# A linear attention followed by a rational feed-forward layer: groups of four d_ff slices by 512 tokens, and the q stage issued beside the MoE stage

## Chip, cores, metric

One core of a Trainium2 chip. The metric is the device time of one execution in microseconds (us), the median of several runs; the profile is of one such run. Engines: PE (TensorE matmul), PEld (its weight loads), DVE (VectorE), ACT (ScalarE), POOL (GpSimd), SP (issues DMAs). "Clock" is the TensorE clock that was granted, as a share of full speed. A "table load" brings a set of function tables to ACT before an Ln or an Exp.

## The reference

```python
# q, k, v: (4 batches, 4 heads, 1088, 32); S1, S2: (8, 32)
phi(x)  = outer(S1 x, S2 x), flattened to 64 features
kv, z   = sum over s of phi(k) v^T, and of phi(k)
x       = (phi(q) kv) / (phi(q) z + 1e-6)          # heads side by side: (4352, 128)
h       = x @ w_in                                  # (4352, 2048)
P       = a0 + a1 h + a2 h^2 + a3 h^3
Q       = 1 + |b0||h| + |b1| h^2
out     = (P / (Q + 1e-6)) @ w_out                  # (4352, 128)
```

## The kernel before

Three stages: k (builds kv for every batch), q (builds x transposed, xT, in SBUF), then MoE (the feed-forward part) over token tiles of 1024. The q stage holds six PSUM banks, which go back before the MoE stage takes eight. The division by Q is Ln and then Exp of the negative, both on ACT. A framework orders each engine's instructions and places their waits; the order on an engine is fixed in the program but is not the order of the source.

```python
    for b in range(B):                                  # the q stage
        for si in range(n_stiles):                      # 9 tiles of 128 tokens
            # load q, transpose (PE), copy (ACT), project (PE), copy (ACT), outer product (DVE)
            for hp in range(H // 2):
                # transpose q_p (PE), copy (ACT), multiply by kv into nd_ps (PE)
                for j in range(2):
                    nc.scalar.copy(out=xT[...], in_=nd_ps[off:off + D, :sl])
                    nc.vector.tensor_copy(out=denb[...], in_=nd_ps[off + D:off + D + 1, :sl])
        for c0 in range(bt0, bt0 + S, CW):              # normalise, 512 tokens at a time
            # reciprocal of denb (DVE), spread over heads (PE, rden_ps), xT *= rden_ps (DVE)
    attn_stack.close()                                  # PSUM of the q stage is given back
    # ... moe_ps 1 x [128,1024] f32, moe_ps_h 2 x [128,1024] f32, moe_ps_t 2 banks
    TT = 1024
    while t0 < n_tok:
        for fi in range(nf):                            # 16 slices of d_ff
            h_ps = moe_ps_h.tile([128, TT], FP, name="h_ps")
            for c0 in range(0, tl, 512):
                nc.tensor.matmul(h_ps[:, c0:c0 + cl], lhsT=w_in_sb[:, fi * 128:(fi + 1) * 128],
                                 rhs=xT_t[:, c0:c0 + cl], start=True, stop=True)
            nc.scalar.copy(out=hh[:, :tl], in_=h_ps[:, :tl])
            # DVE: h2, t1, P3, P (two steps), Qp (two steps)
            nc.scalar.activation(out=habs[:, :tl], in_=hh[:, :tl], func=ACT.Abs, scale=ab0)
            nc.scalar.activation(out=Qln[:, :tl], in_=Qp[:, :tl], func=ACT.Ln, bias=one_ap)
            nc.scalar.activation(out=Qr[:, :tl], in_=Qln[:, :tl], func=ACT.Exp, scale=-1.0)
            nc.vector.tensor_mul(out=g[:, :tl], in0=P[:, :tl], in1=Qr[:, :tl])
            # PE: out_ps += w_out slice @ g; at the end of the tile copy, transpose, copy, store
```

## Time and profile before

| | before |
|---|---|
| time, median | 824.9 us (824.6 to 825.9, 13 runs) |
| k stage, q stage, MoE stage | to 92, 92 to 305, 305 to 823 us |
| ACT busy | 594.5 of 822.9 us |
| table loads on ACT | 159 of 1.283 us |

Two lines of the page of the kernel before: busy us of each engine with its share of the span, and the chain of work that ended last, by engine. They are averages over three stages with different limits; the prediction below takes the stages apart.

```profile
PE 471.7 (57%) x1204; PEld 230.8 (28%) x1212; DVE 422.3 (51%) x892; ACT 594.5 (72%) x905; POOL 9.9 (1%) x55
...
ACT 57%; PE 21%; issue 11%; DVE 8%; DMA 2%; SPq 0%; ACTq 0%
```

ACT leads both, but 72% would suggest much more slack than the MoE stage has.

### The profile page before, as it was taken

Reading aid. Unit: us, or ns where it says so; the run is one execution under the profiler, and the core shown is the slowest. Engines: PE = TensorE matmul, PEld = TensorE weight load, DVE = VectorE, ACT = ScalarE, POOL = GpSimd, SP = SyncE. Lnnn points to the kernel's source line nnn. Section 1 sums busy time; section 2 is a strip of 40 time slices with the busy share of each in tenths; the row PEclk is TensorE's granted clock in tenths of the full one; section 3 lists DMA queues with packets and bytes.
Section 4 is the critical chain, followed back from the end, with each engine's and each line's share of the span. In section 5 each row is a group of like instructions: output and inputs, shape, how many; then the busy total and the mean of one; then the engine's idle time right before and its main releaser. Section 6 shows DMA issues by size and latency. Waiting matters only on the chain.

```text
span 822.9 us, 5049 instructions
## 1 busy us (share of the span) xinstructions
PE 471.7 (57%) x1204; PEld 230.8 (28%) x1212; DVE 422.3 (51%) x892; ACT 594.5 (72%) x905; POOL 9.9 (1%) x55
## 2 busy tenths in 40 slices
PE   3888965665565546555545556554666546533431
PEld 2767733333333222111112111111222212111210
DVE  0111344345434446666566665665656666566333
ACT  2222433332332219999999999999999999999997
POOL 3000000000000000000000000000000000000000
PEclk9999999999999997757676877777555577765555
DMA  6333210000000000000000000000000000000000
GB/s 147 59 59 58 34 28 13 8 11 13 5 0 1 0 0 0 1 0 0 0 6 20 0 1 0 0 20 6 0 0 2 13 13 0 0 0 1 19 7 6
DMA packets 59869, 11.34 MB, mean 14 GB/s; under 512 B 54848, under 2 KB 59200, under 8 KB 59712
## 3 DMA queue, kind: packets, MB, share of 16 engines
q1 hardware_dynamic: 59840, 11.02, 7.1%
q8 instruction: 10, 0.16, 0.1%
q14 instruction: 19, 0.16, 0.1%
HBM read 8.79 MB, written 2.23 MB: 13 GB/s over the span
## 4 chain that ended last, share of the span: by engine, by line
ACT 57%; PE 21%; issue 11%; DVE 8%; DMA 2%; SPq 0%; ACTq 0%
ACT L245 12%; ACT L247 11%; ACT Qln L245 10%; ACT Qr L247 8%; ACT hh L229 7%; PE nd_ps L183 5%; PE kv L134 4%; DVE denb L197 3%; PE ab_ps L126 3%; ACT xT L188 3%; DVE denb L190 3%; ACT habs L237 2%; PE rden_ps L199 2%; PE q_pT L175 2%; PE ab_ps L165 2%
## 5 line engine op out<-in xcount | busy, mean ns | idle before, releaser
L226 PE MATMUL h_ps<-xT,w_in_sb 128*128 128x512 f32 (+1 forms) x288 | 221.7, 892 | 140.2 <-ACT hh L229 139.1
L249 DVE TENSOR_TENSOR g<-P,Qr 128x1024 bf16<-128x1024 bf16 (+1 forms) x80 | 49.0, 612 | 194.8 <-ACT Qr L247 194.8
L226 PEld LDWEIGHTS h_ps<-xT,w_in_sb 128*128 128x128 f32 x288 | 74.5, 280 | 250.6 <-ACT hh L229 207.4
L188 ACT COPY xT<-nd_ps 32x128 f32<-32x128 f32 (+1 forms) x144 | 35.9, 249 | 105.0 <-PE nd_ps L183 77.9
L252 PE MATMUL out_ps<-g,w_out_sb 128*128 128x512 bf16 (+1 forms) x136 | 62.6, 542 | 83.4 <-DVE g L249 83.1
L245 ACT ACT_TABLE_LOAD x79 | 101.4, 1283 | 1.4
L247 ACT ACT_TABLE_LOAD x79 | 101.4, 1283 | 1.4
L190 DVE COPY denb<-nd_ps 1x128 f32<-1x128 f32 (+1 forms) x144 | 40.6, 282 | 84.5 <-ACT xT L188 83.0
L245 ACT ACTIVATE Qln<-Qp,one_ap 128x1024 bf16<-128x1024 bf16 (+1 forms) x80 | 81.5, 1020 | 2.3 <-DVE Qp L243 1.4
L237 ACT ACTIVATE habs<-hh,b_abs 128x1024 bf16<-128x1024 bf16 (+1 forms) x80 | 80.6, 1008 | 0.1
L247 ACT ACTIVATE Qr<-Qln 128x1024 bf16<-128x1024 bf16 (+1 forms) x80 | 74.2, 928 | 0.9
L229 ACT CAST hh<-h_ps 128x1024 bf16<-128x1024 f32 (+1 forms) x80 | 68.8, 868 | 5.6 <-PE h_ps L226 5.6
L183 PE MATMUL nd_ps<-q_pT_sb,kv_blk 128*128 128x128 f32 (+1 forms) x144 | 52.3, 467 | 21.3 <-DVE denb L190 21.3
L252 PEld LDWEIGHTS <-w_out_sb 128*128 128x128 bf16 x144 | 18.6, 131 | 133.5 <-issue 131.8
L130 DVE TENSOR_TENSOR k_p<-ab_sb 128x256 f32<-128x256 f32 (+1 forms) x36 | 15.3, 424 | 75.1 <-ACT ab_sb L128 75.1
L231 DVE TENSOR_TENSOR h<-hh 128x1024 bf16<-128x1024 bf16 (+1 forms) x80 | 48.4, 605 | 5.6 <-ACT hh L229 5.6
L183 PEld LDWEIGHTS nd_ps<-q_pT_sb,kv_blk 128*128 128x128 f32 x144 | 38.6, 321 | 39.1 <-PE q_pT L175 24.4
L175 PE MATMUL q_pT<-ident,q_p 128*128 128x128 f32 (+1 forms) x72 | 33.0, 458 | 28.7 <-ACT q_pT_sb L179 28.1
L243 DVE TENSOR_TENSOR Qp<-Qp,habs 128x1024 bf16<-128x1024 bf16 (+1 forms) x80 | 48.4, 605 | 0.7 <-ACT habs L237 0.6
L240 DVE TENSOR_TENSOR P<-P,t 128x1024 bf16<-128x1024 bf16 (+1 forms) x80 | 48.4, 605 | 0.0
L239 DVE TENSOR_TENSOR P<-P,h 128x1024 bf16<-128x1024 bf16 (+1 forms) x80 | 48.4, 604 | 0.0
L233 DVE TENSOR_SCALAR t<-hh,a_sb 128x1024 bf16<-128x1024 bf16 (+1 forms) x80 | 40.1, 501 | 0.0
(56 smaller groups left out, 468.1 us busy)
## 6 DMA issues: line engine op xcount, KB each, us to landing
out_dram<-outT_sb SPq DMA_DIRECT2D x34, 64.0 KB, 1.6
k_sb<-in_k_dram SPq DMA_DIRECT2D x32, 64.0 KB, 2.3
v_aug<-in_v_dram SPq DMA_DIRECT2D x32, 64.0 KB, 2.1
q_sb<-in_q_dram SPq DMA_DIRECT2D x32, 64.0 KB, 2.0
w_in_sb<-in_moe_w_in_dram SPq DMA_DIRECT2D x1, 1024.0 KB, 5.6
k_sb<-in_k_dram SPq DMA_DIRECT2D x4, 32.0 KB, 2.2
v_aug<-in_v_dram SPq DMA_DIRECT2D x4, 32.0 KB, 2.2
q_sb<-in_q_dram SPq DMA_DIRECT2D x4, 32.0 KB, 2.2
```

The lines of the kernel that those rows point to most:

```text
L175: nc.tensor.transpose(q_pT[:, :sl], in_=q_p[:sl, 2 * hp:2 * hp + 2, :, :].rearrange("s h i j -> s (h i j)"), identity=ident[:sl, :sl])
L183: nc.tensor.matmul(nd_ps[:, :sl], lhsT=kv_blk_sb[:, blk0:blk0 + wblk], rhs=q_pT_sb[:, :sl], start=True, stop=True)
L188: nc.scalar.copy(out=xT[h * D:(h + 1) * D, tok0:tok0 + sl], in_=nd_ps[off:off + D, :sl])
L190: nc.vector.tensor_copy(out=denb[h * D:h * D + 1, tok0:tok0 + sl], in_=nd_ps[off + D:off + D + 1, :sl])
L226: nc.tensor.matmul(h_ps[:, c0:c0 + cl], lhsT=w_in_sb[:, fi * 128:(fi + 1) * 128], rhs=xT_t[:, c0:c0 + cl], start=True, stop=True)
L229: nc.scalar.copy(out=hh[:, :tl], in_=h_ps[:, :tl])
L231: nc.vector.tensor_mul(out=h2[:, :tl], in0=hh[:, :tl], in1=hh[:, :tl])
L237: nc.scalar.activation(out=habs[:, :tl], in_=hh[:, :tl], func=ACT.Abs, scale=ab0)
L245: nc.scalar.activation(out=Qln[:, :tl], in_=Qp[:, :tl], func=ACT.Ln, bias=one_ap)
L247: nc.scalar.activation(out=Qr[:, :tl], in_=Qln[:, :tl], func=ACT.Exp, scale=-1.0)
L249: nc.vector.tensor_mul(out=g[:, :tl], in0=P[:, :tl], in1=Qr[:, :tl])
L252: nc.tensor.matmul(out_ps[:, c0:c0 + cl], lhsT=w_out_sb[:, fi, :], rhs=g[:, c0:c0 + cl], start=(fi == 0), stop=(fi == nf - 1))
```

## The change

Its intent: fewer, longer instructions on ACT and DVE (and fewer table loads) in the MoE stage, and MoE work of one batch beside the q work of the next. The PSUM is split anew so that both fit in eight banks: four for q, one shared by the normalisation and the output transposes, one out_ps, two h_ps of 512.

```diff
-    attn_stack = ExitStack()
-    attn_ps = attn_stack.enter_context(tc.tile_pool(name="attn_ps", bufs=1, ...PSUM))
+    attn_ps = ctx.enter_context(tc.tile_pool(name="attn_ps", bufs=1, ...PSUM))
...
-    attn_ps3 = attn_stack.enter_context(tc.tile_pool(name="attn_ps3", bufs=2, ...PSUM))
+    attn_ps3 = ctx.enter_context(tc.tile_pool(name="attn_ps3", bufs=1, ...PSUM))
...
+    TT = 512
+    def do_moe(t0, tl):
+        NJ = 4
+        for f0 in range(0, nf, NJ):
+            hh = moe_tmp.tile([128, NJ, TT], BF, name="hh")
+            for j in range(NJ):
+                h_ps = moe_ps_h.tile([128, TT], FP, name="h_ps")
+                nc.tensor.matmul(h_ps[:, :tl], lhsT=w_in_sb[:, (f0 + j) * 128:(f0 + j + 1) * 128], ...)
+                nc.scalar.copy(out=hh[:, j, :tl], in_=h_ps[:, :tl])
+            # the same DVE and ACT operations as before, each once over [128, NJ, tl]
...
+    def do_q(b):       # the body of the q loop, unchanged
...
-    attn_stack.close()
+    done = 0
+    do_q(0)
+    for b in range(B):
+        if b + 1 < B:
+            do_q(b + 1)
+        while done < n_tok and min(done + TT, n_tok) <= (b + 1) * S:
+            do_moe(done, min(TT, n_tok - done))
+            done += TT
```

## The prediction

> **What bounds the kernel now.** I read the table of engines by stretches first. It splits the 822.9 us into three stages. The columns are PE, PE weight load, VectorE (DVE), ScalarE (ACT) and GpSimd busy us with instruction counts, then the granted PE clock.
>
> ```profile
> 60.00:80.00 20.00, 17.59 (x105) 14.21 (x105) 3.82 (x9) 4.95 (x22) 1.04 (x10) 1.00 0.37 57
> ...
> 92.00:305.00 213.00, 127.15 (x352) 76.87 (x352) 95.15 (x215) 67.59 (x290) 0.00 (x0) 1.00 0.06 10
> ...
> 310.00:740.00 430.00, 243.86 (x392) 84.25 (x398) 275.81 (x501) 425.78 (x403) 0.00 (x0) 0.69 0.01 4
> ```
>
> The k stage (to 92 us) is PE's, 88% busy. In the q stage (92 to 305 us) nobody is full: PE 60%, DVE 45%, ACT 32%; it is a chain of small steps. In the MoE stage (305 to 823 us) ACT is busy 425.8 of 430 us, 99%. So there ACT's work is the time, and PE has room at a clock of 0.69.
>
> Next the time-ordered view of ACT in the MoE stage: one period, from one Exp to the next, takes 406.80 - 400.04 = 6.76 us.
>
> ```profile
> 400.04 1.06 ACT L247 ACTIVATE Qr<-Qln 128x1024 bf16<-128x1024 bf16 x1
> 401.00 0.99 ACT L229 CAST hh<-h_ps 128x1024 bf16<-128x1024 f32 x1
> 402.01 1.28 ACT L245 ACT_TABLE_LOAD   x1
> 403.30 1.15 ACT L245 ACTIVATE Qln<-Qp,one_ap 128x1024 bf16<-128x1024 bf16 x1
> 404.36 1.13 ACT L237 ACTIVATE habs<-hh,b_abs 128x1024 bf16<-128x1024 bf16 x1
> 405.51 1.28 ACT L247 ACT_TABLE_LOAD   x1
> ```
>
> Two table loads are 2.56 us of the 6.76, and they compute nothing. The order is not the source's: the cast of a later step stands between Exp and Ln, so the steps are already interleaved. Then the groups with shapes kept apart (busy us, mean ns), for two points on the length of each operation:
>
> ```profile
> L245 ACT ACT_TABLE_LOAD x79 | 101.4, 1283 | 1.4
> L247 ACT ACT_TABLE_LOAD x79 | 101.4, 1283 | 1.4
> L245 ACT ACTIVATE Qln<-Qp,one_ap 128x1024 bf16<-128x1024 bf16 x64 | 73.5, 1148 | 2.2 <-DVE Qp L243 1.4
> ...
> L237 ACT ACTIVATE habs<-hh,b_abs 128x1024 bf16<-128x1024 bf16 x64 | 72.7, 1135 | 0.1
> ...
> L229 ACT CAST hh<-h_ps 128x1024 bf16<-128x1024 f32 x64 | 63.3, 996 | 5.6 <-PE h_ps L226 5.6
> ...
> L245 ACT ACTIVATE Qln<-Qp,one_ap 128x256 bf16<-128x256 bf16 x16 | 8.0, 507 | 0.2
> ```
>
> **What the Trainium skill says.** (1) "ScalarE: Activation LUTs", What ACT_TABLE_LOAD costs: 1283 ns a load plus about 1380 ns of drain, 2.66 us a switch. The trace agrees on 1283 and not on the drain: the load at 402.01 starts 0.02 us after the cast before it ends, and Ln starts 0.01 us after the load. I count 1.28 us. (2) The same section gives an ACTIVATE a fixed part (186 ns, about 93 more for each pointer operand) plus 0.833 ns an element, and says that back-to-back ones overlap by about 93 ns. The trace: Ln rises (1148-507)/768 = 0.835 ns an element with 293 ns fixed, and Exp at 400.04 overlaps the cast by 0.10 us. (3) "VectorE: DVE Perf Modes", The TRN2 errata: a fixed cost an instruction, so fewer, longer ones pay it less often. The trace: a bf16 product takes 685 ns at 1024 and 286 at 256, so 153 fixed and 0.52 an element. (4) "TensorE: Matmul & The Clock Gate", The HAM clock gate: half rate after idle windows, full rate after sustained work. The trace shows clocks from 0.50 to 1.00; one 512-wide f32 step (two instructions) takes 1.06 us at full clock (20 instructions in 10.61 us at 305 us) and 2.08 us at the low one (at 402.05).
>
> **The change, part one: bigger groups in the MoE stage.** Before, a step is 1024 tokens by one of 16 slices of d_ff: 5 token tiles (the last of 256) make 80 steps. After, a group is 512 tokens by four slices: 9 token tiles (the last of 256) by 4 are 36 groups, 32 of 2048 elements and 4 of 1024. The casts from PSUM stay one for each 512-wide matmul, 128 + 16 of them. By line through two points:
>
> - Table loads: 158 become 72 (one Ln and one Exp a group), 72 x 1.283 = 92 us, from 203.
> - Ln: 1148 + 1024 x 0.835 = 2003 ns; 32 x 2.003 + 4 x 1.148 = 69 us, from 81.5.
> - Exp: 1911 ns by the same line from 1056 and 415; 65 us, from 74.
> - Abs: 1983 ns from 1135 and 499; 68 us, from 81.
> - Casts: (996-358)/768 = 0.831 an element gives 571 ns at 512; 128 x 0.571 + 16 x 0.358 = 79 us, from 69. This part costs 10 us.
> - Output copies: 14 us, from 13.
>
> Sum 387 us against 521: 134 us less of ACT, 110 of them table loads. A full group on ACT is 4 x 0.571 + 1.983 + 2.003 + 1.911 + 2.566 = 10.75 us for what took two steps or 13.5 us.
>
> On DVE the five products become 42 us each (1217 ns at 2048), the two scale-and-adds 28 each, the scaling 26: 290 us, from 358. A group is 8.4 us of DVE. On PE nothing shrinks: a group has four f32 steps and four bf16 ones (0.29 us at full clock, 0.53 low), 5.4 us at full clock and 10.4 us at half.
>
> **Part two: q work beside MoE work.** The q stage of batch b+1 is now issued ahead of the MoE tiles of batch b, and PSUM is shared out so that both fit. The first normalised chunk (the multiplication into xT) ends at 123 us in the trace before, so MoE work could start there instead of at 305. From 123 to 305 us ACT is busy only 53.5 of 182 us. So after 123 us ACT has 53.5 + 387 = 440 us to do. With no gap it would end at 563, and with the drain of the last group (Exp, product, matmul, copies, transfer: 822.9 - 817.8 = 5 us before) near 570 us.
>
> I don't believe in no gap. Between two batches there are 1088/512 = 2.1 tiles, 8.5 groups: ACT 8.5 x 10.75 + 17 (a batch's q copies, 67.6/4) = 108 us; DVE 8.5 x 8.4 + 24 = 95 us; PE 8.5 x 5.4 + 32 = 78 us at full clock, about 120 with the MoE part at half clock. Three engines are near full, in a fixed order on each. And q is a chain through all three: each half of a tile goes matmul, copy on ACT, copy on DVE, twice, about 2.9 us alone (53 us / 18). Beside 2 us operations on ACT I estimate one more us for each wait on ACT and 0.4 on DVE, so 5.7 us a half and 102 us a batch. That is just the 108 us in which ACT does the MoE work; a little slower, and ACT runs out of MoE work before the next batch is ready. I take ACT at 88% over the three overlapped batches, some 330 us of its work (375 us), and 95% over the last 110 (116 us): 123 + 375 + 116 = 614, less some 10 us for the 0.1 us overlaps of casts that now follow one another, plus 5 of drain. That makes **610 us**.
>
> **The rivals.** (A) **PE becomes the bound.** h_ps shrinks from two buffers of 1024 to two of 512, so PE can run only two matmuls ahead of four casts. At half clock the third and fourth cast each wait 2.08 - 0.57 = 1.5 us: 3 us a group, 36 x 3 = 108 us more, if the casts stand together. For it: the clock is 0.50 at times when PE is busy 6 to 8 of 10 us (580 to 640 us). Against: the order puts single casts between Ln and Exp, and denser work should lift the clock; at 1.00 in the q stage PE does as much. It would make 660 to 700 us. (B) **The overlap fails**: q and MoE merely alternate, because q's chain is stretched or waits for PSUM or for the order on PE. Then the k and q stages keep their 305 us and the MoE stage takes 387 less 10: 690 us. Against: the trace before already mixes the normalisation of one batch with the copies of the next on the same tensors, so the dependence is by slice and not by tensor. (C) **Everything fits** and ACT never waits: 570 us. (D) The loads don't fall, or the groups lose the interleaving, so Ln waits for a DVE chain of about 7 us in each group: 36 x 4 us or more. Two buffers of each tile speak against it, as before.
>
> **Range and chances.** Even where the overlap gives nothing, the loads alone take the time to about 690; only A and B together come near 825. I centre between C and B, nearer to C: 610 us, 570 to 665 for 8 in 10. Faster by over 2% is 0.97, within 2% 0.02, slower 0.01.
>
> **What would show it.** Right: 70 to 73 table loads in all; Ln, Exp and Abs near 2.00, 1.91 and 1.98 us; casts of 0.57 us; ACT busy near 460 us of the span, from 594.5; the first h_ps matmul at 115 to 135 us; PE and DVE busy beside ACT between 130 and 450 us. Wrong: ACT idle for h_ps by tens of us (A); the MoE work starting only after 250 us, or stretches near the ends of batches where ACT is a third busy (B); over 85% ACT in all stretches after 130 us, which would put the time below 590 (C); ACT idle for the Qp of DVE (D).

## The result, and the profile after

631.0 us (629.2 to 632.2, 8 runs) against 824.9. The ratio of the changed kernel to the one before is 0.765 (95% interval 0.764 to 0.7655). Ratios here are the mean time of one kernel's fast runs over that of the other's of the same rounds, so not quite the ratio of the medians quoted.

The same two lines of the page after:

```profile
PE 386.1 (62%) x1200; PEld 205.3 (33%) x1212; DVE 382.7 (61%) x540; ACT 463.7 (74%) x755; POOL 9.9 (2%) x55
...
ACT 52%; PE 36%; DVE 6%; issue 4%; DMA 1%; SPq 0%; ACTq 0%
```

ACT has lost 131 us of work and still leads, but PE's part of the chain has risen from 21% to 36%. The groups with shapes kept apart (busy us, mean ns, then the idle time just before) show where ACT's work went:

```profile
L172 ACT CAST hh<-h_ps 128x512 bf16<-128x512 f32 x128 | 72.6, 586 | 44.5 <-PE h_ps L170 43.9
L180 ACT ACTIVATE habs<-hh,b_abs 128x2048 bf16<-128x2048 bf16 x32 | 64.1, 2004 | 0.3
L188 ACT ACTIVATE Qln<-Qp,one_ap 128x2048 bf16<-128x2048 bf16 x32 | 64.1, 2002 | 2.4 <-DVE Qp L186 2.0
...
L190 ACT ACTIVATE Qr<-Qln 128x2048 bf16<-128x2048 bf16 x32 | 61.1, 1910 | 0.4
...
L188 ACT ACT_TABLE_LOAD x36 | 46.2, 1283 | 0.6
L190 ACT ACT_TABLE_LOAD x36 | 46.2, 1283 | 0.6
```

There are 72 loads in groups, 92.4 us, where there were 158 and 202.8. The last column of the first line is new: the casts wait 43.9 us for h_ps, where before it was 5.6 us in all. The table of stretches after 123 us (where MoE work can begin) shows the cost. Its columns are the length, PE, PEld, DVE, ACT and POOL busy us, the clock, the DMA share and GB/s.

```profile
123.00:500.00 377.00, 230.84 (x583) 106.19 (x592) 274.72 (x376) 318.95 (x477) 0.00 (x0) 0.75 0.03 6
500.00:627.00 127.00, 62.20 (x141) 27.76 (x144) 78.97 (x99) 106.62 (x120) 0.00 (x0) 0.72 0.03 10
```

ACT is busy 425.6 of 504 us, 84%, so 78 us of it idle. What it waited for, as the view of waits has it for 123 to 500 us (us in total, times, longest):

```profile
ACT hh L172 <- PE h_ps L170: 37.3, 37, 2.6
ACT xT L246 <- PE nd_ps L241: 7.3, 10, 3.8
ACT out_sb L198 <- PE out_ps L195: 3.5, 3, 1.2
```

For the rest of the span the wait for h_ps is 10.9 us more: 48 of the 78 us. Finally, the time-ordered view of ACT in the overlapped stage (start us, length, instruction):

```profile
309.48 2.00 ACT L188 ACTIVATE Qln<-Qp,one_ap 128x2048 bf16<-128x2048 bf16 x1
311.50 0.26 ACT L246 COPY xT<-nd_ps 32x128 f32<-32x128 f32 x1
311.78 1.28 ACT L190 ACT_TABLE_LOAD   x1
313.07 1.91 ACT L190 ACTIVATE Qr<-Qln 128x2048 bf16<-128x2048 bf16 x1
315.01 0.25 ACT L246 COPY xT<-nd_ps 32x128 f32<-32x128 f32 x1
...
315.32 1.05 ACT L172 CAST hh<-h_ps 128x512 bf16<-128x512 f32 x2
```

The small q copies sit between the long MoE operations: between these two, ACT spent 3.2 us on a load and an activation, and a q copy that came ready in that time had to wait. In the last line two casts follow each other, which will matter below.

### The profile page after: what moved, and what is told of

Same layout as the page of the kernel before. It is cut to its first block, busy times and chain, and to the rows that moved or that the text cites. A ratio compares the mean times of both kernels' runs of the same rounds, so it can differ in the third digit from the quotient of the medians.

```text
span 627.1 us, 4385 instructions
## 1 busy us (share of the span) xinstructions
PE 386.1 (62%) x1200; PEld 205.3 (33%) x1212; DVE 382.7 (61%) x540; ACT 463.7 (74%) x755; POOL 9.9 (2%) x55
## 4 chain that ended last, share of the span: by engine, by line
ACT 52%; PE 36%; DVE 6%; issue 4%; DMA 1%; SPq 0%; ACTq 0%
PE h_ps L170 14%; ACT Qln L188 11%; ACT Qr L190 10%; ACT L190 7%; ACT L188 6%; PE kv L133 6%; ACT hh L172 5%; ACT habs L180 5%; PE out_ps L195 4%; PE ab_ps L125 4%; ACT xT L246 3%; PE nd_ps L241 2%; ACT q_pT_sb L237 2%; PE kT_ps L116 1%; PE q_pT L233 1%
## 5 line engine op out<-in xcount | busy, mean ns | idle before, releaser
L170 PE MATMUL h_ps<-xT,w_in_sb 128*128 128x512 f32 (+1 forms) x288 | 184.2, 749 | 48.7 <-ACT hh L172 47.1
L172 ACT CAST hh<-h_ps 128x512 bf16<-128x512 f32 (+1 forms) x144 | 78.1, 562 | 48.9 <-PE h_ps L170 48.2
L188 ACT ACTIVATE Qln<-Qp,one_ap 128x2048 bf16<-128x2048 bf16 (+1 forms) x36 | 68.6, 1907 | 2.4 <-DVE Qp L186 2.0
L180 ACT ACTIVATE habs<-hh,b_abs 128x2048 bf16<-128x2048 bf16 (+1 forms) x36 | 68.7, 1908 | 0.4
L192 DVE TENSOR_TENSOR g<-P,Qr 128x2048 bf16<-128x2048 bf16 (+1 forms) x36 | 41.9, 1165 | 39.6 <-ACT Qr L190 39.1
L190 ACT ACTIVATE Qr<-Qln 128x2048 bf16<-128x2048 bf16 (+1 forms) x36 | 65.3, 1815 | 0.4
L174 DVE TENSOR_TENSOR h<-hh 128x2048 bf16<-128x2048 bf16 (+1 forms) x36 | 41.8, 1161 | 8.2 <-ACT hh L172 7.8
L186 DVE TENSOR_TENSOR Qp<-Qp,habs 128x2048 bf16<-128x2048 bf16 (+1 forms) x36 | 41.6, 1155 | 1.1 <-ACT habs L180 0.9
L183 DVE TENSOR_TENSOR P<-P,t 128x2048 bf16<-128x2048 bf16 (+1 forms) x36 | 41.8, 1161 | 0.4
L182 DVE TENSOR_TENSOR P<-P,h 128x2048 bf16<-128x2048 bf16 (+1 forms) x36 | 41.6, 1157 | 0.3
```

Source lines behind the costliest of these rows:

```text
L170: nc.tensor.matmul(h_ps[:, :tl], lhsT=w_in_sb[:, (f0 + j) * 128:(f0 + j + 1) * 128], rhs=xT_t[:, :tl], start=True, stop=True)
L172: nc.scalar.copy(out=hh[:, j, :tl], in_=h_ps[:, :tl])
L174: nc.vector.tensor_mul(out=h2[:, :, :tl], in0=hh[:, :, :tl], in1=hh[:, :, :tl])
L180: nc.scalar.activation(out=habs[:, :, :tl], in_=hh[:, :, :tl], func=ACT.Abs, scale=ab0)
L183: nc.vector.tensor_add(out=P[:, :, :tl], in0=P[:, :, :tl], in1=t1[:, :, :tl])
L188: nc.scalar.activation(out=Qln[:, :, :tl], in_=Qp[:, :, :tl], func=ACT.Ln, bias=one_ap)
```

## The experiments

Each kernel ran beside the kernel before on the same chip, in three rounds; all gave a correct result. Each edit is to the changed kernel unless said otherwise.

### The two parts alone

**groups_h2** and **groups_h6**: bigger groups, no overlap.

```diff
+    for b in range(B): do_q(b)
+    attn_stack.close()              # q's PSUM given back, as before the change
+    moe_ps_h: bufs=2 (groups_h2) or bufs=6 (groups_h6), each [128, 512]; moe_ps_t: bufs=1
+    for t0 in range(0, n_tok, TT): do_moe(t0, min(TT, n_tok - t0))
-    (the look-ahead loop)
```

> Part one alone: the bigger MoE groups, but all q work first and the MoE stage after it as in the kernel before, with h_ps still two buffers of 512. Theory (ACT sets the MoE time, and casts wait for h_ps because only two matmuls can run ahead): MoE work on ACT about 377 us at some 87% busy, so 433 us after 305, in all about 735 us, with 40 us or more of ACT waiting for h_ps. Rival 1 (those waits come only from q work on PE, so without it ACT is 98% busy): about 695 us. Rival 2 (the loads saved bring nothing alone): over 800 us.

> As groups_h2 with six h_ps buffers in place of two, which PSUM has room for when no q work runs. Theory (the depth of h_ps makes the casts wait): the waits for h_ps fall under 15 us and the time is about 695 us, some 40 less than groups_h2. Rival (PE's rate at its low clock, or the order, makes them wait): within 10 us of groups_h2.

Measured: 743.2 us (ratio 0.900) and 694.7 us (0.842). The stretches of the MoE stage and the wait for h_ps in it, first groups_h2, then groups_h6:

```profile
305.00:741.00 436.00, 243.81 (x468) 91.67 (x466) 272.79 (x289) 373.58 (x367) 0.00 (x0) 0.74 0.02 5
...
ACT hh L169 <- PE h_ps L167: 51.8, 40, 2.5
```

```profile
305.00:691.00 386.00, 233.19 (x467) 89.98 (x466) 269.98 (x289) 368.89 (x367) 0.00 (x0) 0.73 0.02 6
...
ACT hh L169 <- PE h_ps L167: 5.5, 4, 4.3
```

ACT's work is nearly the same, the PE clock too; four more buffers take 46 us of waits and 49 us of time away. So more buffers take the wait away at the same clock: with two, PE can't work ahead while ACT is in its long operations. Nor is it that a kinder order parted the casts: in groups_h6 four in a row, at 498.54 us, don't wait. (That the rate of PE plays no part does not follow; bf16_h below shows that it does.) The pair also shows that the h_ps wait needs no q work: it is there without any.

**overlap_nj2**: the overlap alone, with groups the size of the old steps.

```diff
-        NJ = 4
+        NJ = 2
```

> Part two alone: the overlap of q and MoE work as in the changed kernel, with groups of 1024 elements (two slices of d_ff by 512 tokens), the size of a step before, so 144 table loads. Theory: ACT has 185 us of loads and about 508 us of MoE work in all, and 54 of q work after 123 us, 562 us at some 90% busy: about 745 us. Rival (PE and the q chain set the pace of the overlapped stage, not ACT): the table loads cost less than their length there, and the time is under 700 us.

Measured: 732.1 us (0.887), a little under the 745 expected; ACT is busy 539.7 of the 607 us after 123, 89%. The rival (under 700) falls. With two casts a group, and the same two buffers and the same matmul, ACT's wait for h_ps is only 4.8 us. The overlap alone is worth 93 us, the groups alone with the same two buffers 82, and together they are worth 194, 19 more than the sum. "Alone" isn't quite clean: with 512 tokens a tile this kernel has 144 table loads where the one before has 158, so 18 of its 93 us are an estimate of loads saved.

### The order of issue

**q_last**: the same dependences and buffers, with q of the next batch issued after the MoE tiles of this one.

```diff
-    do_q(0)
     for b in range(B):
-        if b + 1 < B:
-            do_q(b + 1)
+        do_q(b)
         while ...: do_moe(...)
```

> The changed kernel with the look-ahead taken out of the issue order: q of batch b+1 is issued after the MoE tiles of batch b in place of before them. Dependences and buffers are the same. Theory (the q chain needs first call on the engines, since it is just as long as the MoE work of a batch): q falls behind, ACT runs dry at the end of each batch, and the time rises to 650 to 690 us. Rival (the overlap comes from the shared PSUM alone, the order of issue does not matter): within 10 us of the changed kernel.

Measured: 674.8 us (0.818), 44 us slower than the changed kernel. The stretches show what was expected, at the end of each batch's MoE work (ACT busy is the fourth of the busy numbers):

```profile
240.00:260.00 20.00, 13.39 (x34) 7.77 (x35) 9.35 (x19) 6.42 (x28) 0.00 (x0) 0.51 0.09 18
...
380.00:400.00 20.00, 14.68 (x36) 7.56 (x35) 9.00 (x18) 7.06 (x25) 0.00 (x0) 0.57 0.00 0
...
500.00:520.00 20.00, 11.75 (x33) 6.63 (x33) 7.47 (x21) 7.49 (x30) 0.00 (x0) 0.50 0.05 14
```

ACT is a third busy there, almost all of it q work, as in the q stage of the kernel before. The casts wait for h_ps as long as in the changed kernel (48.0 us), while ACT's waits for nd_ps and denb, the q chain, are 43 us from 120 us on, against 13. The same tiles and PSUM with another order lose a fifth of the gain, so the look-ahead is a working part of the change.

### What the casts wait for

**bf16_h**: the h matmul in bf16, so PE has far less to do for each cast.

```diff
+    w_in_bf = big.tile([d_model, d_ff], BF); nc.scalar.copy(out=w_in_bf, in_=w_in_sb)
+    xT_bf = big.tile([d_model, n_tok], BF)
-            nc.vector.tensor_mul(out=xT[:, c0:c0 + cl], ...)
+            nc.vector.tensor_mul(out=xT_bf[:, c0:c0 + cl], ...)
     # h_ps <- w_in_bf, xT_bf
```

> The changed kernel with the h matmul in bf16 (w_in is cast once, the normalisation writes xT in bf16), everything else the same: a 512-wide step is then one instruction, some 0.29 us at full clock and 0.53 at half (as out_ps) in place of 1.06 and 2.08. Theory (ACT's idle time after 123 us, 78 us, is mostly casts waiting for a slow PE behind two buffers): the 48 us of waits for h_ps fall under 12, and the time to about 585 us. Rival (the waits come from the fixed order and the q chain on PE, whatever h costs): the waits move to other lines and the time stays over 612.

Measured: 602.4 us (0.730), a gain of 29 us where 46 was expected. ACT's waits from 120 us on:

```profile
ACT xT L249 <- PE nd_ps L244: 15.6, 15, 3.7
ACT hh L175 <- PE h_ps L173: 8.3, 20, 1.2
ACT xT L249 <- DVE denb L251: 7.6, 6, 2.6
```

The stretch after 123 us:

```profile
123.00:601.00 478.00, 218.42 (x592) 95.59 (x592) 353.98 (x474) 425.07 (x596) 0.00 (x0) 0.61 0.03 7
```

The wait for h_ps did what was expected, 48 to 8 us: with two buffers still, a shorter matmul takes it away too, so the wait is made by both together, few buffers and a long matmul. The time lies between the theory (585) and the rival (over 612), and a part of the rival is true: 14 us of idle came back on other lines, 10 of them in the q chain, where the waits for nd_ps and denb in the same window were 13 us in the changed kernel and are 23 here. The clock granted after 123 us fell from 0.74 to 0.61, and an nd_ps matmul of 128 columns became longer, 427 ns on average from 365. So the less busy PE was granted less clock, and its q work got slower; that this makes the 10 us isn't shown.

**h3**: a third h_ps buffer; its bank is won by letting the normalisation and the output transposes use the bank of kT_ps.

```diff
-    moe_ps_h bufs=2                            + moe_ps_h bufs=3
-    outT_ps, rden_ps in attn_ps3 (own bank)    + outT_ps, rden_ps in attn_ps, name="kT_ps"
```

> The changed kernel with three h_ps buffers; the bank comes from letting the normalisation and the output transposes share the bank of kT_ps, which lengthens the q chain a little. Theory (depth matters in the overlapped kernel as it did with the groups alone): waits for h_ps fall from 48 to some 25 us, part of it given back by the shared bank: about 612 us. Rival (with q work between them depth does not matter, PE's rate does): 625 us or more.

Measured: 656.0 us (0.795), 25 us slower than the changed kernel. The theory (612) falls; the time is in the range of the rival (625 or more), but not for its reason, that depth does not matter. ACT's waits from 120 us on:

```profile
ACT xT L245 <- PE nd_ps L240: 47.5, 20, 5.5
ACT hh L171 <- PE h_ps L169: 27.2, 32, 2.6
```

The depth did its part, 48 to 27 us, as expected. But ACT's waits for nd_ps rose from 10 us (in the same window) to 47, and the last normalisation of the q stage came at 561 us, from 517: the q chain got slower. That the shared bank made it so is argued; the edit moves two things at once, and so doesn't price the third buffer by itself either.

### The table loads

The Trainium skill, "ScalarE: Activation LUTs", Table sets, says that one set, natural_log_exp_and_others, holds both functions, so that Ln and Exp need one load. It is not so in either kernel: the traces show 158 loads for the 80 Ln and 80 Exp of the kernel before, and 72 for the 36 and 36 of the changed one. With one load (of set 6) put first, every kernel tried had 1 load in all and a correct result.

**before_oneset** (an edit to the kernel before) and **oneset** (to the changed kernel):

```diff
     nc = tc.nc
+    nc.scalar.add_instruction(mybir.InstLoadActFuncSet(
+        name=nc.get_next_instruction_name(), engine=mybir.EngineType.Activation, act_func_set_id=6))
```

> The kernel before with the one table load put first, so 1 load of 159 is left and nothing else changes. If ACT stayed the bound of the MoE stage, 203 us would go: 622 us. Theory: the stage then runs into DVE and PE: a step is 5.0 us on DVE (5 x 0.685 + 2 x 0.541 + 0.480) and 5.2 us on PE at the low clock, against 4.2 us on ACT, so about 5.3 us a step: 64 x 5.3 + 16 x 2.6 = 381 us after 305, 690 us in all.

> The changed kernel with one table load put first that brings a set with both Ln and Exp, so that 1 load is left of 72 ([...]the result should still agree). It takes 92 us from ACT and nothing else. Theory as predicted (ACT is the bound with 15% idle, PE second): PE and DVE now share the bound and a part of the 92 us comes back as waits for h_ps; about 570 us, with 70 us or more of ACT waiting for h_ps. Rival 1 (ACT alone is the bound): 540 us. Rival 2 (PE and the q chain are the bound already): over 610 us.

Measured: before_oneset 622.9 us (0.755), oneset 532.8 us (0.646). My theory for before_oneset (690 us) fell. The stretch of its MoE stage:

```profile
305.00:621.00 316.00, 194.86 (x468) 76.51 (x467) 304.81 (x641) 286.81 (x359) 0.00 (x0) 0.89 0.03 7
```

DVE is full at 96%, one of the two engines that I named, but a step is shorter than the sum of its durations. The durations of the MoE operations on DVE add up to 358 us and its busy time is 304.8: neighbouring ones overlap by (358 - 305)/640 = 0.08 us. And PE isn't at its low clock: the granted clock rose to 0.89, from 0.66 over the whole MoE stage before, with the same work in less time. That the result is the 622 us of "ACT alone" is chance; ACT is busy 287 of 316 us.

oneset took 98 us off, a little more than the 92 us of loads: the theory (570) falls, and the time is nearest to the rival that ACT alone is the bound (540). The stretch after 123 us:

```profile
123.00:529.00 406.00, 275.20 (x736) 125.78 (x736) 352.97 (x475) 328.50 (x525) 0.00 (x0) 0.82 0.04 8
```

ACT's waits for h_ps are 45 us, no more than before the edit: PE kept up, at a clock of 0.82. DVE is now the busiest, 87%. ACT's busy time after 123 us fell by 97 us, 5 more than the length of the loads. The same shows in the other pairs with and without the loads: 1.35 to 1.38 us of ACT's busy time for each load of 1.28 (before_oneset: 503 to 287 us for 158). Neighbouring activations overlap by some 0.1 us, and a load between them takes that away; that this is the reason is argued, since the order of the instructions changed with the edit too.

**oneset_nj2** (NJ = 2 and the one load), **groups_oneset** (groups_h6 and the one load) and **bf16_oneset** (bf16_h and the one load) fill in the table.

> The overlap with groups of 1024 elements (as overlap_nj2) and the one table load put first. It asks what the bigger groups are worth once no loads are left to save. Theory (nearly all of their worth was loads; what stays is fixed cost on DVE): DVE has 305 us of MoE work (its busy time after 305 us in before_oneset) and 82 of q work after 123 us, some 93% busy: about 540 us, within 20 us of oneset (533). Rival (bigger groups help the overlap in another way, by fewer waits): over 560 us.

> The bigger groups without overlap, six h_ps buffers (as groups_h6), and the one table load put first: ACT has 369 - 92 = 277 us and DVE 270 us of MoE work after 305 us. Theory (two engines both near full, as in before_oneset, where DVE was 97% busy): about 595 us, 28 less than before_oneset (623), so the groups alone are worth that without loads, and the overlap some 60. Rival (the two near-equal engines wait for one another in a chain): 620 us or more.

> The changed kernel with both the one table load and the bf16 h matmul. Theory: DVE is the bound now, 353 us after 123 us at some 92% busy: about 507 us, and waits for h_ps under 12 us. Rival (the q chain through three engines sets the end of each batch, whatever PE and ACT have to do): 525 us or more.

Measured: 556.7 us (0.675), 593.6 us (0.720) and 514.1 us (0.623). For oneset_nj2 neither theory holds quite: it is 24 us above oneset. DVE has 385 us of work after 123 us in place of 353, and ACT waits 24 us for Qp of DVE (8 in oneset) and 35 for nd_ps and denb (13), but only 4 for h_ps (45). How these make the 24 us isn't taken apart. groups_oneset is as expected. bf16_oneset is near its theory (507): DVE busy 352 us of 389, 91%; it is the fastest of all, 38% under the kernel before.

| median us | loads as they are | one load |
|---|---|---|
| before | 824.9 | 622.9 |
| groups alone, h_ps x2 / x6 | 743.2 / 694.7 | not run / 593.6 |
| overlap alone (NJ = 2) | 732.1 | 556.7 |
| the change | 631.0 | 532.8 |
| the change, h in bf16 | 602.4 | 514.1 |

## Why the prediction was right

**ACT's work, term by term.** Predicted and measured: loads 92 and 92.4 us; Ln 69 and 68.6; Exp 65 and 65.3; Abs 68 and 68.7; casts 79 and 78.1. The lines through two sizes gave 2003, 1911 and 1983 ns at 2048; the trace has 2002, 1910 and 2004. ACT's work after 123 us was put at 440 less 10 us and is 425.6.

**The start.** MoE work could start at 123 us: the first weight load for h_ps is at 123.1. Rival B (no overlap, 690 us) is out, and groups_h6, without overlap at 694.7, shows that its number was fair for a kernel whose casts don't wait.

**The q chain beside the MoE work.** Estimated at 102 us a batch against 108 us of ACT work. The last normalisations of the four batches are at 175, 286, 407 and 517 us: 111, 121 and 110 us a batch, 8 to 19 us over the estimate. As both run in one fixed order on each engine, these intervals can't say which of the two set the pace; q_last shows what it costs when q is not given its place.

**The idle share, mis-sized.** "88% over the three overlapped batches" and "95% over the last 110": measured 85% from 123 to 500 us and 84% from there to the end (90% from 520 to 620, so without the drain). That makes 78 us of idle ACT where I had 51 and 5 of drain. These 22 us more, less 4 because ACT's work came out at 426 and not 430, leave 18; the span, 627 us, exceeds 610 by 17 (my terms add up to 609). The rest of the 21 up to 631 lies outside the span of the profiled run. The failing piece is the one called rival A, and its sign, ACT idle for h_ps by tens of us, was on my list. I dismissed it because single casts stood between Ln and Exp in the trace before; but with four casts a group two of them often follow one another, and 47 waits for h_ps cost 48 us, under half of the 108 us that A would have taken. The other argument, that denser work lifts the clock, was worth little: it rose from 0.69 (310 to 740 us before) to 0.74 (after 123 us), and an h_ps instruction still took 775 ns on average, from 919. The wait is there without q work too (groups_h2, 52 us; 11 of the 20 us of idle after 500 us here). It is also why part one alone, put at 134 us of ACT work, is worth 82 us with two buffers and 130 with six.

**The loads.** They were taken as 1.28 us each, without the drain that the skill adds, and this is right in size: before_oneset shows 202 us less for 158 fewer loads. That is no exact measure, since DVE takes over as the bound; the 0.02 us before a load and the 0.01 us after it in the trace are the better one. All five pairs with and without the loads agree in size: 1.22 to 1.40 us less time for each load taken out.

**Not foreseen.** The gain of the change and the gain of one instruction (before_oneset) are equal, 194 and 202 us. The change avoids 86 of 158 loads; all but one were avoidable. I had the table of stages that says ACT's work is the time, and took the loads as given.

## What to carry to other kernels

Where one engine is full, add up its work by operation, and first ask which of it computes nothing: here 203 us were table loads that one load of the right set replaces. Where work of two stages is laid side by side, count its length on every engine and along the longer chain, and issue the chain ahead (44 us here); and count the buffers, since a split of PSUM that makes both fit can make the full engine wait, as two h_ps buffers for four casts did here (46 us, unless the matmul is made shorter). PE may be granted another clock when its work changes (0.61 after 123 us with h in bf16, 0.74 without), so its time in one kernel isn't its time in another.

## What the Trainium skill lacked or had wrong

- "ScalarE: Activation LUTs", What ACT_TABLE_LOAD costs: 2.66 us a switch, drain included. In these traces a load starts 0.02 us after the instruction before it and the activation starts 0.01 us after the load: 1.28 us a switch, and 1.35 to 1.38 us of ACT's busy time for each load taken out.
- The same page, Table sets, says that Ln then Exp take one load. In these kernels nearly every Ln and every Exp had its own (158 loads before, 72 after). The page lacks how to ask for the joint set; one load put first did it (1 load, 202 and 98 us less).
- "TensorE: Matmul & The Clock Gate": the rule of windows doesn't give the clock of a half-busy PE. For the same MoE work it was granted 0.69 in the kernel before (PE 57% busy from 310 to 740 us) and 0.89 in before_oneset (62% from 305 to 621 us); with h in bf16 (46% busy after 123 us) it was 0.61. Nor does the busy share alone give it: q work almost alone was granted 1.00 at 60% busy (kernel before, 92 to 305 us) and 0.51 at 67% (q_last, 240 to 260 us).
